# Regrouped element-wise work, reordered first loads and part of the relu moved to ScalarE in a fused sparse-attention, Fourier and MLP kernel

## The chip, the cores and the metric

The kernel runs on one core of one Trainium2 chip. The metric is device time in microseconds (us). A kernel is run several times; the text gives the median with the lowest and the highest run. A run counts as "slow" when it is more than 1.5% above the fastest of its kernel. Times are compared with the kernel before on the same chip; the traces come from several chips, and of the kernel before there is one.

Engines are written as in the profile: PE is the matrix engine (TensorE), PEld its weight loads, DVE is VectorE, ACT is ScalarE, POOL is GpSimd, SP is SyncE, and "q" after an engine means its queue of issued transfers.

## The reference

Sparse attention with a block gate, then a Fourier mix, a normalisation and an MLP. Cut to what matters:

```python
# q, k, v: batch 4, 8 heads, 768 positions, 64 wide; blocks of 64 positions, so 12 blocks
k_rep = k.reshape(B, H, 12, 64, D).mean(axis=3)
gate  = einsum('bhsd,bhnd->bhsn', q, k_rep)        # then -1e9 where the block lies ahead
sel   = top 3 blocks of gate per query, and the query's own block
scores = q @ k^T / 8, kept where the block is in sel and key <= query
x = softmax(scores) @ v                            # heads side by side: 4 x 768 x 512
u = x + real(fft over positions and features of x)
un = (u - mean(u)) / sqrt(var(u) + 1e-6)
out = u + relu(un @ w1) @ w2                       # w1: 512 x 2048, w2: 2048 x 512
```

## The kernel before

The program handles batches in a pipeline: while attention of batch *b* runs, the Fourier stage and the MLP of batch *b*-1 run beside it, and after batch 3 a tail without attention remains. Attention goes through head pairs. Stage A transposes q and k and forms sums of keys by block, stage B computes gate scores and the top-3 mask, stage C transposes the mask into extra rows of the query operand ("gate columns", 12 rows by 768), stage D computes scores, exponentials, the causal mask on diagonal tiles and the product with v. A scheduler decides the final order on each engine's queue, under the data dependencies; that order is called the built order below.

The loads of batch 0. Query and key tiles have two buffers. The weight loads of the MLP come from POOL behind a "gate": a copy of one element that can't run before pair 2's transposed query exists.

```python
def gen_weights():
    blk_src = attn_P[0][2]["qt"]                    # pair 2 of batch 0
    nc.gpsimd.tensor_copy(out=dummy1[0:1, 0:1], in_=blk_src[0:1, 0:1])   # the gate
    emit_fft_consts()
    for dt in range(NDT):
        nc.gpsimd.dma_start(out=w1_sb[:, dt, 0:DF // 2], ...)    # cut: second half, then w2

def emit_attn_dma(b, hp, ...):                      # cut: v
    qn = apool.tile([128, NST, 2, 64], FP, tag="q_nat", ...)     # the pool has two buffers
    kn = apool.tile([128, NST, 2, 64], FP, tag="k_nat", ...)
    eng = nc.scalar if (b == 0 and hp == 1) else nc.sync
```

The element-wise work of attention: key sums in stage A, the mask in stage B, the diagonal masks in stage D.

```python
# stage A, for each half g of the keys (tp = transposed keys in PSUM, both heads of a pair)
for e in range(2):
    nc.vector.tensor_reduce(out=kr24[64*e:64*e+64, 12*e+6*g:12*e+6*g+6],
                            in_=ps[64*e:64*e+64]..., op=add)
# stage B, for each head e
for st in range(NST):
    nc.vector.max(out=mx8[:, st, :], in_=gsb[:, st, NB*e:NB*(e+1)])
nc.vector.tensor_tensor(out=gm, in0=gsb..., in1=mx8[:, :, 2:3]..., op=is_ge)
nc.vector.tensor_tensor(out=gm, in0=gm, in1=own01, op=max)
nc.vector.tensor_scalar(out=gm, in0=gm, scalar1=1.0, scalar2=-NEG, op0=subtract, op1=mult)
# stage D, for each bank of scores
nc.scalar.activation(out=pt[:, po:po+wid_bank], in_=sp, func=AF.Exp, scale=0.125)
for dof in diags:                                   # each diagonal tile by itself
    nc.vector.tensor_tensor(out=pt[:, dof:dof+128], in0=pt[:, dof:dof+128], in1=ut01, op=mult)
```

The relu of the MLP, 16 times per batch, from PSUM:

```python
nc.vector.tensor_scalar(out=hT[it][:, 0:512],   in0=ha, scalar1=0.0, ..., op0=max)
nc.vector.tensor_scalar(out=hT[it][:, 512:768], in0=hb, scalar1=0.0, ..., op0=max)
```

The softmax here doesn't subtract the row's maximum and nothing guards it: scores larger than these inputs give would overflow.

## Time and profile before

The time was 430.17 us (426.59 to 431.02). The profiled run took 430.97 us, and its span is 429.2 us. The first lines are from the page of the kernel before: busy time of each engine, and the granted TensorE clock in 40 slices of 10.7 us, in tenths of full speed.

```profile
PE 359.6 (84%) x2638; PEld 229.9 (54%) x2638; DVE 313.2 (73%) x1079; ACT 169.7 (40%) x355; POOL 39.1 (9%) x59
PEclk9655555768957999999969999999789999989999
```

PE is busy for 84% of the span, but not always at full speed: slices three to seven stand near 5, half speed. The average also hides stages with different limits, so here is the windows view of the same kernel, cut at marks that the trace gives: first score, last product with v of batch 0, then batch 3's first half (until PE transposes the normalised rows, ahead of the MLP), its second half, and the tail. The columns are the window, its length, busy time and instruction count of PE, PEld, DVE, ACT and POOL, the granted clock, the DMA share and GB/s.

```profile
0.00:42.90 42.90, 22.33 (x100) 17.41 (x101) 15.60 (x78) 13.33 (x27) 19.47 (x35) 0.67 1.20 188
42.90:81.70 38.80, 37.01 (x285) 24.93 (x282) 24.87 (x119) 29.25 (x59) 4.92 (x6) 0.53 0.70 96
257.50:310.40 52.90, 44.48 (x278) 26.88 (x275) 44.77 (x158) 27.11 (x58) 1.34 (x2) 0.95 0.28 64
310.40:348.50 38.10, 37.74 (x380) 25.91 (x381) 32.48 (x107) 13.98 (x31) 0.00 (x0) 0.94 0.00 1
348.50:429.20 80.70, 70.98 (x400) 37.76 (x396) 45.91 (x98) 4.70 (x8) 0.00 (x0) 0.97 0.11 40
```

Four readings follow. The first 42.9 us are waiting for data: PE is busy for 22.3 of them. The stretch to 81.7 us is PE-bound at a clock of 0.53. In the first half of batch 3 PE stands still for 52.90 - 44.48 = 8.4 us. In the second half PE is busy for 37.7 of 38.1 us, so nothing that DVE or ACT does there can matter unless it makes PE wait.

What holds the first 42.9 us is in the chain of waits (the chain of work that ended last; start, length, what). Pieces of it up to the first exponential:

```profile
13.99 0.87 PE tp_0_0_0_192 L230 x3
...
16.81 0.37 SPq L179
...
17.23 16.78 DMA qn_2_179<-in_q_dram
...
34.14 0.87 PE tp_2_0_0_300 L230 x3
...
43.49 1.28 ACT L300
...
```

Pair 0's transposes start at 14.0 us. When they are done, SP issues pair 2's query load (line 179) into the freed buffer, and that load takes 16.8 us; pair 2's transposes start at 34.1 us. The 1.28 us on ACT is a table load right ahead of the first exponential (ACT_TABLE_LOAD, line 300, 1283 ns).

The view of PE's waits shows the wait for the gate columns, once per batch (line, waited for, us in total, times, longest):

```profile
PE tp_2_0_0_300 L230 <- DMA qn_2_179<-in_q_dram: 11.0, 1, 11.0
PE sc_1_0_0_1406 L293 <- DVE qg_1_0_1034 L276: 4.7, 1, 4.7
...
PE sc_1_0_0_3898 L293 <- DVE qg_1_0_3469 L276: 4.2, 1, 4.2
```

### The profile page before, as it was taken

The page shows a single profiled execution, that of the slowest core. Times are in us where ns is not written, and L with a number is a line of the kernel's source. Part 1 is how long each engine was busy: PE and PEld are TensorE (multiplying, and loading weights), DVE is VectorE, ACT ScalarE, POOL GpSimd, SP SyncE. Part 2 cuts the span into 40 slices and gives each one's busy share as a digit, 9 for nine tenths or more (in the row PEclk, how much of TensorE's full clock was granted, in tenths as well). Part 3 has the DMA queues.
Part 4 walks back from the last instruction along what each step waited for, and adds up shares of the span by engine and source line. Part 5 has one row for each costly group of instructions (what it writes and reads, how often), then busy time and mean ns, then how long its engine had stood idle before and what let it go on. Part 6 is the DMA issues. An engine that isn't in the chain of part 4 may idle for free.

```text
span 429.2 us, 7093 instructions
## 1 busy us (share of the span) xinstructions
PE 359.6 (84%) x2638; PEld 229.9 (54%) x2638; DVE 313.2 (73%) x1079; ACT 169.7 (40%) x355; POOL 39.1 (9%) x59
## 2 busy tenths in 40 slices
PE   6518999667659999998599998999599999959996
PEld 2417666445427666465456664666276655536542
DVE  0436666759896989688989889589979893777611
ACT  1513967736851440443763323635624402010000
POOL 6703012200001111000000111000000000000000
PEclk9655555768957999999969999999789999989999
DMA  9999972725302115444302227410000001100021
GB/s 159 213 201 180 195 106 19 96 43 120 74 0 20 13 9 37 124 124 99 98 2 20 19 20 118 122 51 25 2 2 1 2 2 73 52 23 2 0 75 73
DMA packets 84627, 28.04 MB, mean 65 GB/s; under 512 B 78032, under 2 KB 80304, under 8 KB 84592
## 3 DMA queue, kind: packets, MB, share of 16 engines
q0 software_dynamic: 28832, 8.48, 18.3%
q1 hardware_dynamic: 52416, 18.28, 17.7%
q10 hardware_dynamic: 3344, 0.82, 1.1%
q8 instruction: 21, 0.34, 0.3%
q14 instruction: 14, 0.11, 0.1%
HBM read 28.62 MB, written 6.29 MB: 81 GB/s over the span
## 4 chain that ended last, share of the span: by engine, by line
PE 67%; DVE 20%; DMA 7%; ACT 4%; issue 2%; SPq 0%; ACTq 0%
DMA qn_2_179<-in_q_dram 4%; DMA qn_1_137<-in_q_dram 2%; PE ch_5_3691 L481 1%; PE ch_5_2445 L481 1%; PE ch_5_5142 L481 1%; PE ch_5_4730 L481 1%; PE ch_4_4699 L481 1%; PE ch_3_5104 L481 1%; PE ch_2_5085 L481 1%; PE ch_0_5047 L481 1%; PE ch_3_4668 L481 1%; PE ch_2_4627 L481 1%; PE ch_0_4553 L481 1%; PE ch_4_3586 L481 1%; PE ch_3_3555 L481 1%
## 5 line engine op out<-in xcount | busy, mean ns | idle before, releaser
L466 PEld LDWEIGHTS <-w_sb 128*128 128x128 f16 x256 | 25.1, 98 | 25.7 <-issue 0.3
L467 PEld LDWEIGHTS <-w_sb 128*128 128x128 f16 x256 | 25.0, 98 | 6.0 <-issue 0.7
L188 POOL DMA_DIRECT2D v_0_0_89<-in_v_dram x4 | 3.4, 857 | 120.4 <-PE av_0_0_2736 L317 56.0
L293 PEld LDWEIGHTS <-kI_1_82 76*128 76x128 f16 x32 | 4.2, 134 | 14.3 <-issue 5.3
L230 PE MATMUL tp_2_0_0_300<-id_72,qn_2_179 128*128 128x128 f32 x3 | 0.9, 430 | 11.0 <-DMA qn_2_179<-in_q_dram 11.0
L140 ACT COPY unT_0_4797<-unt_0_4807 128x768 f16<-128x768 f16 x1 | 0.8, 798 | 20.3 <-PE unt_0_4807 L455 20.3
L293 PEld LDWEIGHTS <-kI_1_86 76*128 76x128 f16 x32 | 4.1, 130 | 8.6 <-issue 6.3
L121 PE MATMUL warmps<-warm_src 128*128 128x512 f16 x22 | 6.5, 467 | 1.2 <-DVE v_0_2_91 L131 1.2
L383 PE MATMUL yp_0_997<-fs_sb,fg_989 128*128 128x193 f16 x6 | 1.2, 364 | 7.7 <-DVE fg_989 L371 7.7
L383 PEld LDWEIGHTS <-fg_989 128*128 128x128 f16 x24 | 2.4, 117 | 8.7 <-DVE fg_989 L371 7.9
L394 ACT CAST yg_0_4606<-yp_0_4599 128x386 f16<-128x386 f32 x1 | 0.6, 598 | 15.0 <-PE yp_0_4599 L383 15.0
L188 POOL DMA_DIRECT2D v_0_1_90<-in_v_dram x4 | 3.3, 826 | 34.6 <-PE av_1_0_1721 L317 12.4
L230 PEld LDWEIGHTS tp_2_0_0_300<-id_72,qn_2_179 128*128 128x128 f32 x3 | 0.5, 212 | 11.1 <-issue 11.1
L235 DVE COPY qT_0_2_295<-tp_2_0_0_300 128x384 f32<-128x384 f32 x1 | 0.6, 557 | 8.0 <-PE tp_2_0_0_300 L230 8.0
L455 PE MATMUL unt_0_4807<-id_73,x_3300 128*128 128x128 f16 x6 | 1.7, 288 | 5.3 <-DVE x_3300 L448 5.3
L230 PE MATMUL tp_0_0_0_192<-id_72,qn_0_97 128*128 128x128 f32 x3 | 0.9, 430 | 6.2 <-DMA qn_1_137<-in_q_dram 6.2
L188 POOL DMA_DIRECT2D v_0_2_91<-in_v_dram x4 | 3.3, 828 | 28.7 <-PE av_2_0_3152 L317 10.8
L239 ACT CAST kI_2_83<-tp_2_1_0_314 64x384 f16<-64x384 f32 x1 | 0.5, 472 | 13.0 <-PE tp_2_1_0_314 L230 13.0
L235 DVE COPY qT_0_0_187<-tp_0_0_0_192 128x384 f32<-128x384 f32 x1 | 0.6, 558 | 6.9 <-PE tp_0_0_0_192 L230 6.9
L236 ACT CAST qg_0_0_188<-tp_0_0_0_192 64x384 f16<-64x384 f32 x1 | 0.5, 472 | 12.7 <-DMA kn_1_138<-in_k_dram 12.7
L455 PEld LDWEIGHTS <-x_3300 128*128 128x128 f16 x24 | 2.1, 130 | 6.3 <-DVE x_3300 L448 5.8
L239 ACT CAST kI_0_81<-tp_0_1_0_2124 64x384 f16<-64x384 f32 x1 | 0.5, 472 | 12.0 <-PE tp_0_1_0_2124 L230 12.0
(2598 smaller groups left out, 1347.3 us busy)
## 6 DMA issues: line engine op xcount, KB each, us to landing
w_sb<-in_moe_w_ch_dram POOLq DMA_DIRECT2D x8, 256.0 KB, 10.4
w_sb<-in_moe_w_ch_dram POOLq DMA_DIRECT2D x4, 512.0 KB, 13.5
out_dram<-u_939 SPq DMA_DIRECT2D x6, 256.0 KB, 2.4
out_dram<-u_2071 SPq DMA_DIRECT2D x6, 256.0 KB, 2.0
out_dram<-u_3317 SPq DMA_DIRECT2D x6, 256.0 KB, 2.0
out_dram<-u_4546 SPq DMA_DIRECT2D x6, 256.0 KB, 2.0
fs_sb<-c_FS POOLq DMA_DIRECT2D x1, 582.0 KB, 6.5
qn_0_97<-in_q_dram SPq DMA_DIRECT2D x4, 96.0 KB, 4.7
```

What stands on the lines that cost most here:

```text
L121: nc.tensor.matmul(wps, wsrc[:, 0:128], wsrc, start=True, stop=True)
L140: eng.copy(out=dst, in_=src)
L188: nc.gpsimd.dma_start(out=v16_t[e][sl][:, :, 0:64], in_=v[b, h].rearrange("(jt p) d -> p jt d", p=128))
L230: nc.tensor.transpose(ps[:, i, :], src[:, st, :, :].rearrange("p h d -> p (h d)"), id32)
L235: nc.vector.tensor_copy(out=qt[:, cols], in_=flat)
L239: nc.scalar.copy(out=kI[0][0:64, cols], in_=flat[0:64])
L293: nc.tensor.matmul(sp[:, co:co + (a1 - a0)], kI[e][0:76, 128 * jt:128 * (jt + 1)], qg[e][0:76, a0:a1], start=True, stop=True)
L383: nc.tensor.matmul(out_p, fg[:, 3 * par + st, 128 * g:128 * (g + 1)], fs_sb[:, g % 2, par, st, 0:KQ], start=(st == 0), stop=(st == 2))
L455: nc.tensor.transpose(tps[:, st, :], un16[:, st, 128 * dt:128 * (dt + 1)], id16)
L466: nc.tensor.matmul(ha, w1s, unT[dt][:, 0:512], start=(dt == 0), stop=(dt == NDT - 1))
L467: nc.tensor.matmul(hb, w1s, unT[dt][:, 512:768], start=(dt == 0), stop=(dt == NDT - 1))
L481: nc.tensor.matmul(cps, hT[it][:, 128 * st:128 * (st + 1)], w2_sb[:, it, :], start=(it == 0), stop=(it == NIT - 1))
```

## The change

Its intent is to start attention earlier, to take work from DVE by doing the same element-wise work in fewer and larger instructions, and to give ACT two thirds of the relu (512 of 768 columns). The core of the diff (cut: constants, pools, index bookkeeping):

```diff
 # loads
-            qn = apool.tile([128, NST, 2, 64], FP, tag="q_nat", name=...)      # and kn
-            eng = nc.scalar if (b == 0 and hp == 1) else nc.sync
+            qn = apool.tile([128, NST, 2, 64], FP, tag="q_nat", name=..., bufs=3)
+            # q on SP's queue, k on ACT's queue in batch 0; pairs 0, 1, 2 issued up front
-    emit_attn_dma(0, 0, qk_only=True)
     emit_priority_consts()
-    emit_attn_dma(0, 1, qk_only=True)
+    for hp in range(3):
+        emit_attn_dma(0, hp, qk_only=True)
+    emit_rest_consts()
 # key sums: both heads in one reduce, then spread by a 0/1 table
-                        for e in range(2):
-                            nc.vector.tensor_reduce(out=kr24[64*e:64*e+64, ...], ...)
+                        nc.vector.tensor_reduce(out=kr12[:, 6*g:6*g+6], in_=ps..., op=add)
+            nc.vector.tensor_tensor(out=kr24..., in0=kr12...to_broadcast([128, 2, NB]),
+                                    in1=half24..., op=mult)
 # top-3 mask: both heads at once, two operations for six
-                nc.vector.tensor_tensor(out=gm, ..., op=is_ge)
-                nc.vector.tensor_tensor(out=gm, in0=gm, in1=own01, op=max)
-                nc.vector.tensor_scalar(out=gm, ..., op0=subtract, op1=mult)
+            nc.vector.tensor_tensor(out=g4, in0=g4, in1=mx8[..., 2:3]..., op=is_lt)
+            nc.vector.scalar_tensor_tensor(out=gmp..., in0=g4, scalar=NEG, in1=other24...,
+                                           op0=mult, op1=mult)
 # scores: diagonal tiles side by side, so that one multiply masks up to four
-        [(0, 0, 512)],
-        [(0, 512, 768), (4, 512, 768)],                              # cut
+        [(0, 0, 128), (1, 128, 256), (2, 256, 384), (3, 384, 512)],
+        [(4, 512, 640), (5, 640, 768), (4, 640, 768), (0, 128, 256)],  # cut
-                    for dof in diags:
-                        nc.vector.tensor_tensor(out=pt[:, dof:dof+128], ..., in1=ut01, op=mult)
+                    if ndiag:
+                        nc.vector.tensor_tensor(out=dg, in0=dg,
+                            in1=ut01...to_broadcast([128, ndiag, 128]), op=mult)
 # relu of the first 512 columns
-            nc.vector.tensor_scalar(out=hT[it][:, 0:512], in0=ha, scalar1=0.0, ..., op0=max)
+            nc.scalar.activation(out=hT[it][:, 0:512], in_=ha, func=AF.Relu)
```

More of the change, by code (lines that the diff above doesn't have):

```diff
@@ L54, in _consts_np @@
     cz24 = np.concatenate([cz, cz], axis=1)
-    own01 = ((s // 64)[:, None] == nn[None, :]).astype(np.float16)
+    other = ((s // 64)[:, None] != nn[None, :]).astype(np.float32)
+    other24 = np.concatenate([other, other], axis=1)
+    half24 = ((jj[:, None] // 64) == (np.arange(2 * NB)[None, :] // NB)).astype(np.float32)
     IndR = (nn[:, None] == (s[None, :] // 64)).astype(np.float16)
     return dict(FS=FS, FD=FD, ident32=ident32, ident16=ident16,
-                ltri=ltri, ut01=ut01, cz24=cz24, own01=own01, IndR=IndR)
+                ltri=ltri, ut01=ut01, cz24=cz24, other24=other24, half24=half24, IndR=IndR)
 @with_exitstack
@@ L90 @@
     bpool = ctx.enter_context(tc.tile_pool(name="bat", bufs=1))
-    spool = ctx.enter_context(tc.tile_pool(name="small", bufs=8))
+    spool = ctx.enter_context(tc.tile_pool(name="small", bufs=4))
     def pst(shape, name, dtype=FP, tag="ps", bufs=None):
@@ L101 @@
     cz24 = cpool.tile([128, NST, 2 * NB], FP, tag="c_cz24", name="cz24")
-    own01 = cpool.tile([128, NST, NB], F16, tag="c_own", name="own01")
+    other24 = cpool.tile([128, NST, 2 * NB], FP, tag="c_other", name="other24")
+    half24 = cpool.tile([128, 2 * NB], FP, tag="c_half", name="half24")
     eps1 = cpool.tile([128, 1], FP, tag="c_eps1", name="eps1")
@@ L113, in emit_priority_consts @@
         nc.sync.dma_start(id32, dr["ident32"].ap())
-        nc.sync.dma_start(id16, dr["ident16"].ap())
+        nc.gpsimd.dma_start(id16, dr["ident16"].ap())
         nc.vector.memset(eps1, 1e-6)
@@ L124, in emit_rest_consts @@
     def emit_rest_consts():
-        nc.sync.dma_start(cz24, dr["cz24"].ap().rearrange("(st p) n -> p st n", p=128))
-        nc.sync.dma_start(own01, dr["own01"].ap().rearrange("(st p) n -> p st n", p=128))
-        nc.scalar.dma_start(ut01, dr["ut01"].ap())
+        nc.gpsimd.dma_start(cz24, dr["cz24"].ap().rearrange("(st p) n -> p st n", p=128))
+        nc.gpsimd.dma_start(half24, dr["half24"].ap())
+        nc.gpsimd.dma_start(other24, dr["other24"].ap().rearrange("(st p) n -> p st n", p=128))
+        nc.gpsimd.dma_start(ut01, dr["ut01"].ap())
         for e in range(2):
@@ L168, in emit_attn_dma @@
         if not v_only:
-            qn = apool.tile([128, NST, 2, 64], FP, tag="q_nat", name=f"qn_{b}_{hp}")
-            kn = apool.tile([128, NST, 2, 64], FP, tag="k_nat", name=f"kn_{b}_{hp}")
-            eng = nc.scalar if (b == 0 and hp == 1) else nc.sync
-            nsp = 2 if (b == 0 and hp < 2) else 1
-            for e in range(2):
-                h = 2 * hp + e
-                for part in range(nsp):
-                    s0, s1 = part * (NST // nsp), (part + 1) * (NST // nsp)
-                    eng.dma_start(qn[:, s0:s1, e, :],
-                                  q[b, h, 128 * s0:128 * s1].rearrange("(st p) d -> p st d", p=128))
-                    eng.dma_start(kn[:, s0:s1, e, :],
-                                  k[b, h, 128 * s0:128 * s1].rearrange("(st p) d -> p st d", p=128))
+            qn = apool.tile([128, NST, 2, 64], FP, tag="q_nat", name=f"qn_{b}_{hp}", bufs=3)
+            kn = apool.tile([128, NST, 2, 64], FP, tag="k_nat", name=f"kn_{b}_{hp}", bufs=3)
+            for (t, src, eng) in ((qn, q, nc.sync), (kn, k, nc.scalar if b == 0 else nc.sync)):
+                for e in range(2):
+                    eng.dma_start(t[:, :, e, :], src[b, 2 * hp + e]
+                                  .rearrange("(st p) d -> p st d", p=128))
             P.setdefault(hp, {})["qn"] = qn
@@ L191 @@
     BANKS = [
-        [(0, 0, 512)],
-        [(0, 512, 768), (4, 512, 768)],
-        [(1, 128, 640)],
-        [(1, 640, 768), (3, 384, 768)],
-        [(2, 256, 768)],
-        [(5, 640, 768)],
+        [(0, 0, 128), (1, 128, 256), (2, 256, 384), (3, 384, 512)],
+        [(4, 512, 640), (5, 640, 768), (4, 640, 768), (0, 128, 256)],
+        [(0, 256, 768)],
+        [(1, 256, 768)],
+        [(2, 384, 768), (3, 512, 640)],
+        [(3, 640, 768)],
     ]
-    OFF = {}
+    COL = {}
     PT_W = 0
@@ L202 @@
         for (jt, a0, a1) in bank:
-            if jt not in OFF:
-                OFF[jt] = PT_W - (a0 - 128 * jt)
+            for i in range(a0, a1, 128):
+                COL[jt, i // 128] = PT_W + i - a0
             PT_W += a1 - a0
-    assert PT_W == 2688
+    assert PT_W == 2688 and len(COL) == 21
     def gen_attention(b):
@@ L217, in stage_A @@
             qt = apool.tile([128, S], FP, tag="qT32", name=f"qT32_{b}_{hp}")
-            qg = [apool.tile([128, S], F16, tag=f"qg{e}", name=f"qg_{b}_{hp}_{e}", bufs=4)
+            qg = [apool.tile([128, S], F16, tag=f"qg{e}", name=f"qg_{b}_{hp}_{e}", bufs=3)
                   for e in range(2)]
@@ L221, in stage_A @@
             kr24 = apool.tile([128, 2 * NB], FP, tag="kr24", name=f"kr24_{b}_{hp}")
-            nc.vector.memset(kr24, 0.0)
+            kr12 = apool.tile([128, NB], FP, tag="kr12", name=f"kr12_{b}_{hp}")
             d["qt"], d["qg"], d["kI"], d["kr24"] = qt, qg, kI, kr24
@@ L240, in stage_A @@
                         nc.scalar.copy(out=kI[1][0:64, cols], in_=flat[64:128])
-                        for e in range(2):
-                            nc.vector.tensor_reduce(
-                                out=kr24[64 * e:64 * e + 64, 12 * e + 6 * g:12 * e + 6 * g + 6],
-                                in_=ps[64 * e:64 * e + 64].rearrange("p a (x c) -> p a x c", x=2),
-                                axis=mybir.AxisListType.X, op=mybir.AluOpType.add)
+                        nc.vector.tensor_reduce(
+                            out=kr12[:, 6 * g:6 * g + 6],
+                            in_=ps.rearrange("p a (x c) -> p a x c", x=2),
+                            axis=mybir.AxisListType.X, op=mybir.AluOpType.add)
+            nc.vector.tensor_tensor(out=kr24.rearrange("p (e n) -> p e n", e=2),
+                                    in0=kr12.rearrange("p (o n) -> p o n", o=1)
+                                    .to_broadcast([128, 2, NB]),
+                                    in1=half24.rearrange("p (e n) -> p e n", e=2),
+                                    op=mybir.AluOpType.mult)
         def stage_B(hp):
@@ L254, in stage_B @@
             nc.vector.tensor_tensor(out=gsb, in0=gps, in1=cz24, op=mybir.AluOpType.add)
-            gmp = apool.tile([128, NST, 44], F16, tag="gmp", name=f"gmp_{b}_{hp}", bufs=4)
+            gmp = apool.tile([128, NST, 64], F16, tag="gmp", name=f"gmp_{b}_{hp}", bufs=4)
             d["gmp"] = gmp
-            for e in range(2):
-                gm = gmp[:, :, 32 * e:32 * e + NB]
-                mx8 = spool.tile([128, NST, 8], FP, tag="mx8", name=f"mx8_{b}_{hp}_{e}")
-                for st in range(NST):
-                    nc.vector.max(out=mx8[:, st, :], in_=gsb[:, st, NB * e:NB * (e + 1)])
-                nc.vector.tensor_tensor(out=gm, in0=gsb[:, :, NB * e:NB * (e + 1)],
-                                        in1=mx8[:, :, 2:3].to_broadcast([128, NST, NB]),
-                                        op=mybir.AluOpType.is_ge)
-                nc.vector.tensor_tensor(out=gm, in0=gm, in1=own01, op=mybir.AluOpType.max)
-                nc.vector.tensor_scalar(out=gm, in0=gm, scalar1=1.0, scalar2=-NEG,
-                                        op0=mybir.AluOpType.subtract, op1=mybir.AluOpType.mult)
+            mx8 = spool.tile([128, NST, 2, 8], FP, tag="mx8", name=f"mx8_{b}_{hp}", bufs=4)
+            for st in range(NST):
+                for e in range(2):
+                    nc.vector.max(out=mx8[:, st, e, :], in_=gsb[:, st, NB * e:NB * (e + 1)])
+            g4 = gsb.rearrange("p s (e n) -> p s e n", e=2)
+            nc.vector.tensor_tensor(out=g4, in0=g4,
+                                    in1=mx8[:, :, :, 2:3].to_broadcast([128, NST, 2, NB]),
+                                    op=mybir.AluOpType.is_lt)
+            nc.vector.scalar_tensor_tensor(
+                out=gmp.rearrange("p s (e n) -> p s e n", e=2)[:, :, :, 0:NB], in0=g4, scalar=NEG,
+                in1=other24.rearrange("p s (e n) -> p s e n", e=2),
+                op0=mybir.AluOpType.mult, op1=mybir.AluOpType.mult)
         def stage_C(hp):
@@ L273, in stage_C @@
             for st in range(NST):
-                nc.tensor.transpose(gt[0:44, st, :], gmp[:, st, :], id16)
+                nc.tensor.transpose(gt[0:44, st, :], gmp[:, st, 0:44], id16)
             for e in range(2):
@@ L290, in stage_D_scores @@
                     co = 0
-                    diags = []
+                    ndiag = 0
                     for (jt, a0, a1) in bank:
@@ L297, in stage_D_scores @@
                         if a0 == 128 * jt:
-                            diags.append(po + co)
+                            ndiag += 1
                         co += a1 - a0
@@ L301, in stage_D_scores @@
                                          scale=0.125)
-                    for dof in diags:
-                        nc.vector.tensor_tensor(out=pt[:, dof:dof + 128], in0=pt[:, dof:dof + 128],
-                                                in1=ut01, op=mybir.AluOpType.mult)
+                    if ndiag:
+                        dg = pt[:, po:po + 128 * ndiag].rearrange("p (n c) -> p n c", c=128)
+                        nc.vector.tensor_tensor(
+                            out=dg, in0=dg,
+                            in1=ut01.rearrange("p (o c) -> p o c", o=1)
+                            .to_broadcast([128, ndiag, 128]),
+                            op=mybir.AluOpType.mult)
                 po += wid_bank
@@ L317, in stage_D_av @@
                         nc.tensor.matmul(av[:, st, 0:65],
-                                         pt[:, OFF[jt] + 128 * (st - jt):OFF[jt] + 128 * (st - jt) + 128],
+                                         pt[:, COL[jt, st]:COL[jt, st] + 128],
                                          v16[e][:, jt, 0:65],
@@ L328, in gen_attention @@
         if b > 0:
-            emit_attn_dma(b, 0, qk_only=True)
-            emit_attn_dma(b, 1, qk_only=True)
-            emit_attn_dma(b, 0, v_only=True)
-            emit_attn_dma(b, 1, v_only=True)
+            for hp in range(3):
+                emit_attn_dma(b, hp, qk_only=True)
+            for hp in range(3):
+                emit_attn_dma(b, hp, v_only=True)
             yield
@@ L335, in gen_attention @@
             if i < NP:
-                if i + 2 < NP:
+                if 1 <= i and i + 2 < NP:
                     emit_attn_dma(b, i + 2)
@@ L467, in gen_post @@
                 nc.tensor.matmul(hb, w1s, unT[dt][:, 512:768], start=(dt == 0), stop=(dt == NDT - 1))
-            nc.vector.tensor_scalar(out=hT[it][:, 0:512], in0=ha, scalar1=0.0, scalar2=None,
-                                    op0=mybir.AluOpType.max)
+            nc.scalar.activation(out=hT[it][:, 0:512], in_=ha, func=AF.Relu)
             nc.vector.tensor_scalar(out=hT[it][:, 512:768], in0=hb, scalar1=0.0, scalar2=None,
@@ L498, in drive @@
             gens = alive
-    emit_attn_dma(0, 0, qk_only=True)
     emit_priority_consts()
-    emit_attn_dma(0, 1, qk_only=True)
+    for hp in range(3):
+        emit_attn_dma(0, hp, qk_only=True)
+    emit_rest_consts()
     emit_attn_dma(0, 0, v_only=True)
     emit_attn_dma(0, 1, v_only=True)
-    emit_rest_consts()
+    emit_attn_dma(0, 2, v_only=True)
     def gen_weights_delayed(nskip):
```

## The prediction

> **What bounds the kernel now.** The span (429.2 us), from the windows view and the chain of waits:
>
> - 0 to 44 us, loads. The first transposes start at 14.0 us; those of head pair 2 wait for its query load (16.8 us in the chain) until 34.1. That load starts only when pair 0's buffer is free, and shares the DMA engines with the MLP weights.
> - 44 to 80 us, attention of batch 0: PE busy 36.2 of 38 us at granted clock 0.53.
> - 80 to 166, 166 to 257, 257 to 348 us: attention of batch b beside Fourier and MLP of b-1. Each has a first half (batch 3: 51.5 us, PE 43.2, DVE 43.4 busy) whose chain alternates between DVE and PE, and a second half (39.5 us, PE 39.0) that is PE alone. Batch 1's first half is DVE-bound (DVE 40.0 of 46, PE 27.2).
> - 348 to 429 us, tail without attention: PE, a short DVE chain, PE.
>
> **What the change does.** The Fourier stage does not change. The rest:
>
> 1. Loads: the identity first, q and k on two queues, three buffers, so pair 2 is fetched at once. In the built order the weight gate now stands before all eight first weight loads (before, seven stood ahead of it). At the 160 to 210 GB/s of the first slices (estimate), pair 0 lands near 7 us, pair 2 near 17, pair 3 near 23. PE's order still puts pair 3's transposes before the first score, so scores start near 25 instead of 43.5 us. The 36.7 us after that keep their length if the clock stays low. Gain 18 us.
> 2. Key sums: 64 reduces of 553 ns become 32 plus 16 small multiplies: about 4 us of DVE per batch. Masks: 192 multiplies of 220 ns become 64; from 128 columns 220 ns, 762 columns 553, 1536 columns 954 I estimate 420 ns (512 columns) and 290 (256). [...] Top-k mask: six operations become two. Together 6 us of DVE per batch in the first halves, about 4 of it in the chain. Gain 4 us each for batches 2 and 3, 5 for batch 1.
> 3. Relu: 64 x 690 ns go from DVE to ACT (about 600 ns each, by exponentials of that size). [...] the built order keeps two table loads. It lies in the PE-bound half and gains almost nothing; relus beside bursts of twelve exponentials (one per 0.48 us) may stall PE 0.5 us a burst. Cost 1 to 2 us in all.
> 4. Scores: 8 matmuls per head become 13, most 128 columns wide; one takes 54 ns start to start, so no loss.
>
> The tail stays at 81 us.
>
> **Predicted: 400 us**, 389 to 412 in 8 of 10 cases. Faster by over 2%: 0.97; within 2%: 0.025; slower: 0.005.
>
> **What would show it.** Step 1: first score near 25 us, batch 0 ending near 62. Step 2: DVE busy down from 313 to 235-250 us (relu included), PE's 4.2 us wait for the gate columns shorter, first halves about 47 us. Step 3: ACT busy near 205 us, second halves 39 to 41 us, short new waits of PE on ACT's relu.
>
> **What would make it wrong.** The clock: it stood at half speed from 32 to 90 us although PE was busy; at full clock batch 0 would end up to 8 us earlier. Pair 3's load or the values could come late. Relu behind exponentials could cost more.

430 us, less 18 for the loads and 13 for the element-wise work (5 + 4 + 4), plus 1 to 2 for the relu, comes to 400 to 401. Its 420 and 290 ns for grouped masks are the estimate from the three durations it names; these lie near 155 ns plus 0.52 ns per column.

## More of the kernel before

The chain at the end of batch 3's first half is a chain on DVE. These pieces lie between the gate scores (PE, line 251) and the first of the diagonal masks behind them:

```profile
299.20 1.27 PE g_2_3811 L251 x12
...
302.51 0.45 DVE kr_3_3_3779 L242
302.97 0.56 DVE kr_3_3_3779 L242
303.54 0.55 DVE kr_3_3_3779 L242
304.11 0.56 DVE kr_3_3_3779 L242
...
304.97 0.56 DVE qg_1_0_3469 L276
...
307.49 0.11 DVE ptl_1_0_3896 L303
```

The four key-sum reduces (line 242) take 0.45 to 0.56 us each, one after the other, ahead of the gate columns (qg, line 276) that PE's scores wait for. The diagonal masks (ptl, line 303) contribute five pieces of 0.11 to 0.13 us. Over the whole of this first half, key sums take 5.4 us of the chain (summed over its pieces).

## The result, and the profile after

The changed kernel took 399.54 us (398.69 to 406.64, four runs); the kernel before took 428.83 us (426.59 to 431.02) beside it. The ratio is 0.932 (95% interval 0.926 to 0.938). Ratios here and below are the mean time of one kernel's fast runs over that of the other's fast runs of the same rounds, so not quite the ratio of the quoted medians.

The first profile of the changed kernel fell in a slow run (406.64 us, mean clock 0.873; the fast runs had 0.90). The comparison below uses a profile of the same kernel in a fast run (398.40 us, clock 0.903), taken in a later set of runs. The page's busy times and clock in that run:

```profile
PE 351.8 (89%) x2798; PEld 231.1 (58%) x2798; DVE 244.4 (62%) x791; ACT 203.9 (51%) x419; POOL 42.5 (11%) x64
PEclk9655997985799999997799999997799999989999
```

DVE lost 68.8 us and ACT gained 34.2 us. The clock row has fewer fives early on. The windows view of this kernel, cut at the same marks:

```profile
0.00:27.60 27.60, 22.61 (x100) 16.32 (x101) 11.16 (x65) 13.35 (x27) 17.12 (x31) 0.73 1.37 180
27.60:58.90 31.30, 28.15 (x325) 21.52 (x322) 19.20 (x74) 26.95 (x59) 10.57 (x15) 0.80 1.23 213
227.60:277.20 49.60, 44.12 (x294) 27.85 (x292) 39.27 (x131) 26.82 (x58) 1.29 (x2) 0.95 0.23 53
277.20:315.70 38.50, 38.26 (x401) 26.87 (x402) 21.58 (x64) 22.95 (x47) 0.00 (x0) 0.93 0.01 1
315.70:396.60 80.90, 70.95 (x398) 37.77 (x396) 36.11 (x82) 14.26 (x24) 0.00 (x0) 0.97 0.11 40
```

The gain lies in three places. The first score comes 15.3 us earlier. The stretch after it is 7.5 us shorter, at a clock of 0.80 where it was 0.53. The first half of batch 3 is 3.3 us shorter, of which 2.9 us is less standing still of PE (49.60 - 44.12 = 5.5 us in place of 8.4). The second half and the tail moved by 0.4 and 0.2 us, although DVE is 10.9 us less busy in that second half: this PE-bound stage did not notice. Summed over the span: batch 0 gave 22.8 us (its end moved from 81.7 to 58.9), batches 1 to 3 gave 10.0 (266.8 to 256.8), the tail took 0.2.

The chain of waits at the start, for the changed kernel:

```profile
2.83 8.80 DMA qn<-in_q_dram
...
14.82 2.55 PE g L253 x12
...
20.28 0.47 DVE kr L239
...
21.70 2.59 PE g L253 x12
...
29.16 1.28 ACT L303
...
```

No load stands in the chain after 11.6 us. From there it is transposes, gate scores and copies, with PE at half clock: the twelve gate-score passes take 2.55 us here, where the clock row stands at 6 and 5, and 1.27 us at full clock (in the chain of batch 3, and as long in the kernel before, at a granted clock of 1.00 from 299.2 to 300.5 us). And the end of batch 3's first half:

```profile
267.43 1.27 PE g L253 x12
...
269.69 0.87 DVE mx L262 x12
270.59 0.55 DVE qg L279
271.17 0.56 DVE kr L239
...
271.94 0.47 DVE kr L239
...
272.73 0.56 DVE qg L279
...
273.34 3.83 PE sc L296 x18
```

Two key-sum reduces stand where four stood, and PE starts its scores 4.6 us after the gate scores ended (5.1 us before). Over the whole first half, key sums take 1.7 us of the chain where they took 5.4. PE's waits for gate columns are now several short ones (7 times, 2.1 us the longest; their sum fell from 15.1 to 10.4 us), and the wait for pair 2's query is gone; what is left of waiting for queries is 2.0 us:

```profile
PE sc L296 <- DVE qg L279: 10.4, 7, 2.1
PE tp L228 <- DMA qn<-in_q_dram: 2.0, 1, 2.0
PE sc L296 <- ACT ptl L303: 1.9, 2, 1.7
```

### The profile page after: what moved, and what is told of

It is laid out like the page before. It is cut to its first block, busy times and chain, and to the rows that moved or that the text cites. A ratio compares the mean times of both kernels' runs of the same rounds, so it can differ in the third digit from the quotient of the medians.

```text
span 404.9 us, 7205 instructions
## 1 busy us (share of the span) xinstructions
PE 358.5 (89%) x2798; PEld 236.2 (58%) x2798; DVE 244.7 (60%) x791; ACT 205.5 (51%) x419; POOL 42.5 (11%) x64
## 4 chain that ended last, share of the span: by engine, by line
PE 74%; DVE 13%; ACT 5%; DMA 4%; issue 2%; POOL 0%; ACTq 0%; SPq 0%; POOLq 0%
DMA cz_75<-c_cz 2%; DMA kI_1_87<-c_IndR 2%; DMA qn_0_2017<-in_q_dram 1%; PE ch_5_3624 L487 1%; PE ch_1_3339 L487 1%; PE ch_5_2394 L487 1%; PE ch_1_2109 L487 1%; PE ch_5_5072 L487 1%; PE ch_5_4660 L487 1%; PE ch_2_5015 L487 1%; PE ch_4_5053 L487 1%; PE ch_3_5034 L487 1%; PE ch_1_4996 L487 1%; PE ch_0_4977 L487 1%; PE ch_4_4629 L487 1%
## 5 line engine op out<-in xcount | busy, mean ns | idle before, releaser
L296 PEld LDWEIGHTS <-kI_1_83 76*128 76x128 f16 x52 | 5.5, 131 | 8.9 <-issue 3.6
L296 PEld LDWEIGHTS <-kI_1_87 76*128 76x128 f16 x52 | 5.2, 128 | 7.8 <-DVE qg_1_1_1012 L279 2.4
L296 PEld LDWEIGHTS <-kI_0_86 76*128 76x128 f16 x52 | 4.9, 112 | 3.4 <-issue 2.7
L186 POOL DMA_DIRECT2D v_0_2_92<-in_v_dram x4 | 3.3, 822 | 28.0 <-PE av_2_0_1868 L324 10.9
L296 PEld LDWEIGHTS <-kI_2_88 76*128 76x128 f16 x52 | 4.6, 108 | 2.7 <-issue 1.2
L296 PEld LDWEIGHTS <-kI_3_89 76*128 76x128 f16 x52 | 4.6, 107 | 2.2 <-issue 0.7
L296 PEld LDWEIGHTS <-kI_0_82 76*128 76x128 f16 x52 | 5.0, 114 | 1.4 <-issue 0.9
L124 PEld LDWEIGHTS <-warm_src 128*128 128x128 f16 x22 | 2.6, 121 | 5.1 <-issue 2.7
L296 PEld LDWEIGHTS <-kI_3_85 76*128 76x128 f16 x52 | 4.7, 108 | 1.2
L296 PEld LDWEIGHTS <-kI_2_84 76*128 76x128 f16 x52 | 4.6, 108 | 1.3 <-issue 0.2
L228 PE MATMUL tp_1_0_0_228<-id_72,qn_1_134 128*128 128x128 f32 x3 | 0.9, 430 | 4.4 <-DMA qn_1_134<-in_q_dram 4.4
```

Of the source, the lines that this page charges most:

```text
L124: nc.tensor.matmul(wps, wsrc[:, 0:128], wsrc, start=True, stop=True)
L186: nc.gpsimd.dma_start(out=v16_t[e][sl][:, :, 0:64], in_=v[b, h].rearrange("(jt p) d -> p jt d", p=128))
L228: nc.tensor.transpose(ps[:, i, :], src[:, st, :, :].rearrange("p h d -> p (h d)"), id32)
L296: nc.tensor.matmul(sp[:, co:co + (a1 - a0)], kI[e][0:76, 128 * jt:128 * (jt + 1)], qg[e][0:76, a0:a1], start=True, stop=True)
```

## The experiments

The total was near what was predicted, so the question was whether its parts were. The theory was the prediction's: 18 us from the loads, 13 from the element-wise work, a small cost from the relu. The main rivals were that the loads give less than that and the element-wise work more; that the loads gain by no longer sharing the DMA engines with the MLP's weights, not by being issued earlier; and that a large part is the clock of batch 0, which is not the change's doing at all. All runs gave correct results. This table collects what the traces of the profiled runs show; "first score" is the time of PE's first score, "stretch" is from there to the end of batch 0, "batches 1-3" is their sum, all in us.

| kernel | median time | before, same chip | first score | stretch | end of batch 0 | batches 1-3 | tail |
|---|---|---|---|---|---|---|---|
| before | 428.83 | - | 42.9 | 38.8 | 81.7 | 266.8 | 80.7 |
| changed (after_third) | 398.53 | 428.21 | 27.6 | 31.3 | 58.9 | 256.8 | 80.9 |
| changed (its first profile, slow) | 399.54 | 428.83 | 30.3 | 35.6 | 65.8 | 257.0 | 82.1 |
| loads_only | 420.31 | 428.72 | 31.9 | 37.5 | 69.4 | 267.6 | 81.7 |
| gate_only | 421.00 | 428.21 | 33.4 | 37.3 | 70.8 | 267.1 | 81.4 |
| elem_again | 411.23 | 428.21 | 36.9 | 34.5 | 71.4 | 257.5 | 80.6 |
| kr_only | 418.03 | 428.21 | 40.0 | 37.6 | 77.6 | 258.7 | 82.4 |
| diag_only | 423.47 | 427.90 | 42.5 | 30.2 | 72.7 | 268.4 | 80.7 |
| relu_only | 428.35 | 428.72 | 42.5 | 33.0 | 75.5 | 266.3 | 82.3 |
| no_relu | 399.53 | 428.86 | 28.9 | 31.1 | 60.1 | 256.9 | 80.9 |
| after_ungated | 404.89 | 427.90 | 28.1 | 35.6 | 63.6 | 256.9 | 82.1 |
| c_first_exp | 394.43 | 427.90 | 22.7 | 34.2 | 56.9 | 254.4 | 82.6 |

Of the columns, the first score and batches 1-3 are steady where kernels share the code that sets them (for instance 266.3 to 268.4 in all kernels without the new key sums). The stretch is not: 33.0 in relu_only and 38.8 in the kernel before, which have the same code there; the granted clock of the stretch is 0.79 in the one and 0.53 in the other.

### The changed kernel again, loads alone, element-wise work alone, relu alone

after_again is the changed kernel without an edit.

> The changed kernel unchanged, for a profile in the fast state (the first one fell in a slow run of 406.6 us against 398.7 to 400.3). Both theories: 397 to 401 us. If the 7 us between its slow and fast runs is the clock of TensorE in batches 0 and 1, the fast profile shows the same order of work and the same waits, with fewer half-speed stretches before 140 us; if it is the DMA, the first score comes earlier than 30.3 us.

The median was 398.23 us against 428.72 us. Three runs took 397.6 to 398.5 us, and the fourth, which was the profiled one, 428.55 us at a mean clock of 0.787. In that run the clock was not lost early only: from 107 us to the end of the program its clock row stands at 8 in every slice but three (5, 5 and 6), where the fast profile mostly has 9, and the 512-column matmuls of the MLP take 419 to 422 ns on average in place of 379. PE is busy for 384.0 us in place of 351.8, DVE and ACT for 246.2 and 203.8 in place of 244.4 and 203.9. It shows how far a lower clock can carry the time with the same code, up to the time of the kernel before; it says nothing on the change. Because of it the interval of the ratio was wide (0.936, 0.920 to 0.952), and the kernel was run once more below.

loads_only has the part of the diff that concerns loads (three buffers, q and k on two queues, pairs 0 to 2 up front, constants on POOL's queue), with the old element-wise work and relu:

```diff
-            qn = apool.tile([128, NST, 2, 64], FP, tag="q_nat", name=...)
+            qn = apool.tile([128, NST, 2, 64], FP, tag="q_nat", name=..., bufs=3)
+    for hp in range(3):
+        emit_attn_dma(0, hp, qk_only=True)      # and the other load edits of the change
```

> The kernel before with the new loads alone (one load per head, q and k on two queues, constants on the third, three buffers). Theory: the loads give 12 to 15 us: about 415 us, first score near 30 us instead of 42.9, batch 0 over near 67 us instead of 81.4, and the three batches and the tail keep their lengths (85, 91, 91, 81 us). Rival (batch 0 is bound by TensorE at half clock, so an earlier start is given back): at most 5 us, 424 us or more.

It took 420.31 us (420.05 to 420.56) against 428.72: 8.4 us by medians. The ratio is 0.988 with an interval that includes 1 (0.971 to 1.004), because only two of the seven runs of the kernel before counted as fast. The result lies between the theory and its rival, as the median gain is 8.4 us where 12 to 15 or at most 5 were expected. The trace is clear where the clock of the stretch doesn't enter: the first score comes at 31.9 us in place of 42.9. Batches 1 to 3 did not move (267.6 against 266.8). Why the first score comes 4.3 us later than in the changed kernel, with the same loads, is in the chain of waits of loads_only:

```profile
2.84 9.47 DMA qn<-in_q_dram
...
14.47 0.54 DVE kr L236
15.03 0.56 DVE kr L236
...
16.89 2.74 PE g L245 x12
...
```

No load stands in it after 12.3 us. Up to the first exponential it holds eight old key-sum reduces (4.4 us in all), where the changed kernel's chain holds one new one of 0.47 us.

elem_only has the new key sums, mask and diagonal grouping, with the old loads of q, k and v and the old relu (the diff of the change's second, third and fourth part; it also loads the new constants and keeps the change's smaller pools):

```diff
+                        nc.vector.tensor_reduce(out=kr12[:, 6*g:6*g+6], in_=ps..., op=add)
+            nc.vector.tensor_tensor(out=g4, in0=g4, in1=mx8[..., 2:3]..., op=is_lt)
+            nc.vector.scalar_tensor_tensor(out=gmp..., op0=mult, op1=mult)
+                        nc.vector.tensor_tensor(out=dg, in0=dg, in1=ut01...to_broadcast(...), op=mult)
```

> The kernel before with the regrouped attention element-wise work alone (key sums, top-k mask, score banks with grouped diagonals); old loads, relu on DVE. Theory: about 3 us in each of batches 1 to 3 and 2 us in batch 0, 417 to 420 us, DVE busy near 285 us. Rival (the batches became shorter because relu left DVE): 426 us or more.

Three runs took 408.6 to 413.5 us, faster than the 417 to 420 expected. The fourth, the profiled one, took 685.07 us: the mean of the 512-column matmuls was 677 to 680 ns where it is 379 ns in the changed kernel's fast profile. Its trace holds no clock record (the page has no clock row, and the 1.0 listed for the run is what the tool gives without one), so it doesn't show what clock was granted. It can't be compared with anything, and the same kernel went again as elem_again.

relu_only moves the relu of 512 columns to ACT and does nothing else:

```diff
-            nc.vector.tensor_scalar(out=hT[it][:, 0:512], in0=ha, scalar1=0.0, ..., op0=max)
+            nc.scalar.activation(out=hT[it][:, 0:512], in_=ha, func=AF.Relu)
```

> The kernel before with two thirds of the relu on ACT alone. Theory: the relu lies in the halves that PE bounds, so nothing is gained: 427 to 431 us, DVE busy near 272 us, ACT near 206 us. Rival (DVE relieved of 40 us is the gain of the batches): 420 us or less.

It took 428.35 us against 428.72 (ratio 1.007, 0.991 to 1.023). One relu takes 691 ns on DVE and 625 ns on ACT. The windows view of relu_only, the second half of batch 3:

```profile
303.70:341.80 38.10, 37.81 (x380) 25.95 (x381) 24.09 (x91) 22.86 (x47) 0.00 (x0) 0.94 0.00 1
```

DVE fell from 32.5 to 24.1 us and ACT rose from 14.0 to 22.9, and the window is 38.10 us as it was, with PE busy for 37.8. The time is the one that the theory gave. The feared stall of PE behind ACT did not appear: no wait on the relu is among PE's waits in that profile.

### The fast profile, element-wise work again, key sums alone, and the weight gate alone

after_third is the changed kernel once more.

> The changed kernel once more, for a profile of a fast run (two profiles fell in slow ones). Theory: its fast runs (397 to 400 us) differ from the first profile (404.9 us) by the clock in batch 0: the scores of batch 0 then last about 30 us instead of 35.6, the halves of batches 1 to 3 are the same as there within 0.5 us. Rival: the difference is in the tail or in the loads.

It took 398.53 us (398.40 to 399.25) against 428.21, ratio 0.933 (0.926 to 0.940). Its profile is the one shown in the result. The theory, that only the clock of batch 0 sets the slow profile apart, holds in part: of the 8.3 us between the two spans, 4.3 lie in the stretch (clock 0.58 against 0.80), but 2.6 lie before the first score and 1.2 in the tail.

elem_again is the kernel of elem_only.

> The element-wise part alone once more, as its profile fell in a run of 685 us with all matmuls slowed. It gave 17 us where 9 to 12 were expected. Theory A: the halves of batches 1 to 3 shorten by 3.3 us each as in the whole change, and the rest comes in batch 0, where the weight gate of the built order now stands after four weight loads instead of seven, so that pair 2's queries land about 4 us earlier, and where a higher clock is granted: batch 0 ends near 74 us instead of 81.7. Theory B: the regrouping itself is worth more than thought: batches 1 to 3 shorten by 5 us each or more.

It took 411.23 us (409.16 to 414.53), ratio 0.963 (0.955 to 0.972): 17.0 us by medians. Theory A fits the trace. Batches 1 to 3 gave 9.3 us (266.8 to 257.5). And batch 0 gave 10.3 us (81.7 to 71.4), with no edit in the code of the q, k, v and weight loads. Of these, 6.0 lie before the first score (36.9 us in place of 42.9) and 4.3 in the stretch, at a clock of 0.60 in place of 0.53. Most of the 6.0 goes with the built order of POOL's queue. In the kernel before, seven weight loads stand ahead of the gate; in this one, four. Pair 2's transposes start at 29.6 us in place of 34.1. An edit in DVE's work thus changed how many transfers compete with pair 2's query.

kr_only has the new key sums alone:

```diff
-                        for e in range(2):
-                            nc.vector.tensor_reduce(out=kr24[64*e:64*e+64, ...], ...)
+                        nc.vector.tensor_reduce(out=kr12[:, 6*g:6*g+6], in_=ps..., op=add)
+            nc.vector.tensor_tensor(out=kr24..., in0=kr12..., in1=half24..., op=mult)
```

> The kernel before with the key sums alone changed (one reduce for both heads and a masking multiply). Theory: two thirds of the gain of the regrouping in the batches: first halves of batches 2 and 3 at 50.5 to 51 us instead of 52.9. The weight gate stands after five loads, so pair 2 should come 2 to 3 us earlier: 419 to 424 us. If the halved number of reduces meant nothing: first halves 52.9 us as before.

It took 418.03 us (416.18 to 420.69), ratio 0.977 (0.967 to 0.987). Batches 1 to 3 take 258.7 us, so the key sums alone give 8.1 of the 10.0 us that the whole change gives there. That leaves about 1 us for the top-k mask and the diagonals together (elem_again: 257.5); the mask was not run alone. In the chain of batch 3's first half, key sums fell from 5.4 to 1.2 us. The windows view, batch 3's first half in kr_only:

```profile
247.60:297.70 50.10, 43.71 (x275) 27.00 (x274) 40.25 (x151) 26.54 (x57) 1.27 (x2) 0.96 0.29 68
```

PE stands still for 6.4 us where it stood for 8.4. The half is 50.1 us long, a little less than the 50.5 to 51 expected. Five weight loads stand ahead of the gate here, and pair 2's transposes start at 31.6 us.

gate_only keeps the old loads, with two buffers and the old order, and makes the gate hold. In the kernel before, the weight loads share no data with the gate's copy, so the scheduler may put them ahead of it. Here POOL copies one element of pair 2's transposed query into each tile that a weight load then overwrites, so each load has to come after:

```diff
-        nc.gpsimd.tensor_copy(out=dummy1[0:1, 0:1], in_=blk_src[0:1, 0:1])
+        for dt in range(NDT):
+            for c in (0, DF // 2):
+                nc.gpsimd.tensor_copy(out=w1_sb[0:1, dt, c:c + 1], in_=blk_src[0:1, 0:1])
+        for c in range(4):
+            nc.gpsimd.tensor_copy(out=w2_sb[0:1, 4 * c, 0:1], in_=blk_src[0:1, 0:1])
```

> The kernel before with one thing changed: every load of the MLP weights really waits for pair 2's queries to be transposed. Theory (contention): pair 2's queries land by 24 us instead of 34, the first score starts near 33 us instead of 42.9, about 419 us. Rival (the late issue for want of a third buffer is the cause): pair 2's transposes still start after 31 us, 426 us or more.

It took 421.00 us (414.74 to 422.26), ratio 0.978 (0.963 to 0.993). Its profiled run is labelled slow, being 1.5% above a single fast run of 414.74 us; its clock (0.869) is that of most runs of the kernel before (0.86 to 0.87), so it is a fair trace to read loads from. The chain of waits of gate_only:

```profile
17.19 0.37 SPq L183
...
17.61 7.07 DMA qn<-in_q_dram
24.81 2.17 PE tp L234 x9
...
34.16 1.28 ACT L304
...
```

The issue stands where it stood (17.2 us; 16.8 before), into the same two buffers. The load takes 7.07 us where it took 16.78, as the theory of contention said. The gain of gate_only (7.2 us) and that of loads_only (8.4 us) are the same within the spread of the runs. So what held pair 2 back was mainly competition with the weights for the DMA engines (in the kernel before, the DMA share is 1.08 while the load runs, from 17.2 to 34.0 us, at 225 GB/s): with the weights away, its transposes start at 24.8 us in place of 34.1. The late issue after pair 0's buffer cost less: with the new loads alone they start at 20.0 us, and the first score comes 1.5 us ahead of gate_only's (31.9 against 33.4). The weights are issued by POOL and the query by SP, so in these two traces separate queues did not keep them apart. Across the two-buffer kernels, the start of pair 2's transposes follows the number of weight loads ahead of the gate: 33.7 to 34.1 us with seven (three kernels), 31.6 with five, 29.6 with four, 24.8 with none.

### Diagonals alone, the change without its gate, and a version meant to be faster

diag_only has the regrouped score banks and the grouped diagonal masks alone:

```diff
-        [(0, 0, 512)],
-        [(0, 512, 768), (4, 512, 768)],                              # cut
+        [(0, 0, 128), (1, 128, 256), (2, 256, 384), (3, 384, 512)],
+        [(4, 512, 640), (5, 640, 768), (4, 640, 768), (0, 128, 256)],  # cut
-                    for dof in diags: ...                            # 6 multiplies per head
+                    if ndiag: ...                                    # 2 multiplies per head
```

> The kernel before with the score banks and the grouped diagonal masks alone (192 masks of 220 ns become 64). The key sums gave 2.8 of the 3.2 us per batch, so theory: DVE busy falls by 10 us or more and nothing is gained in the batches: first halves 52.3 to 52.9 us, second halves 38 to 38.6, at most 1 us slower from the narrower score matmuls. What moves in batch 0 is the weight gate's place in the built order (seven loads before it, as in the kernel before), so 425 to 430 us. Rival (the prediction: all DVE work of the first halves counts alike): first halves near 51.5 us.

It took 423.47 us (422.39 to 424.84), ratio 0.990 (0.983 to 0.997). The windows view, batch 3's first half in diag_only:

```profile
250.10:302.80 52.70, 44.34 (x295) 27.88 (x292) 44.60 (x149) 26.85 (x58) 1.34 (x2) 0.95 0.28 65
```

DVE lost 10.5 us in all (313.2 to 302.7), but 0.2 us in this window, and the window is 52.70 us where it was 52.90. Batches 1 to 3 together are 1.6 us longer than before, not shorter; the lengthening is in batch 1's first half (48.3 in place of 46.5 us), at a clock of 0.67 in place of 0.77. As expected, then, nothing is gained in the batches; that the total came out under the 425 to 430 us expected is due to the stretch of batch 0 (30.2 in place of 38.8 us), at a clock of 0.80 in place of 0.53. All four runs of diag_only have that clock (0.877 to 0.884, against 0.853 to 0.893 before). Whether the regrouping causes it is open.

after_ungated is the changed kernel without the gate:

```diff
-        blk_src = attn_P[0][2]["qt"]
-        nc.gpsimd.tensor_copy(out=dummy1[0:1, 0:1], in_=blk_src[0:1, 0:1])
```

> The changed kernel without the gate of the weight loads. The gate alone gave the kernel before all that the new loads gave it. Theory: with three buffers the queries of pair 2 are issued at 2 us, before any weight load can start (near 18 us on its queue), so only pair 3 can suffer: first score 27.6 to 30 us, 398 to 402 us. Rival (the gate is the gain): first score after 33 us, 405 us or more.

It took 404.89 us (399.91 to 405.40), ratio 0.944 (0.937 to 0.950). The first score is at 28.1 us, against 27.6. But the run is no test of the gate: with the constants and the values ahead of them on POOL's queue, the first weight load is issued at 22.6 us without the gate and at 22.3 with it, and pair 2's transposes start at 17.7 and 17.8 us, earlier than either. So the gate did not hold anything back in the changed kernel, and whether an early issue would do with the weights issued at 16 us, as in the kernel before, no run shows. The time missed the 398 to 402 us expected. The 6 us are in the stretch: 35.6 us against 31.3, at a clock of 0.58 against 0.80:

```profile
28.10:63.60 35.50, 33.44 (x324) 25.82 (x322) 19.24 (x74) 28.48 (x59) 10.58 (x15) 0.58 1.30 207
```

The changed kernel's own first profile has the same 35.6 us, and one run of after_ungated (399.91 us, clock 0.904) was as fast as the changed kernel. So both kernels can land in either case, although their loads are the same in time; three of four runs of after_ungated landed in the slower one, and one of twelve of the changed kernel (406.64 us; its 428.55 us run is left out). Why is open.

c_first_exp is the changed kernel with two edits. Stage C is emitted ahead of stages A and B of the same step, so that the gate columns of a pair do not queue on DVE behind the key sums of a later pair. And the early dummy activation is Exp in place of Ln, so that the exponential's table is loaded while the first loads run, not right ahead of the first exponential:

```diff
-        nc.scalar.activation(out=dummy1, in_=eps1, func=AF.Ln, bias=eps1)
+        nc.scalar.activation(out=dummy1, in_=eps1, func=AF.Exp)
         for i in range(NP + 3):
+            if 0 <= i - 2 < NP:
+                stage_C(i - 2)
             if i < NP:
                 ...
                 stage_A(i)
             if 0 <= i - 1 < NP:
                 stage_B(i - 1)
-            if 0 <= i - 2 < NP:
-                stage_C(i - 2)
```

> The changed kernel with two small edits: in each step the gate columns of an older head pair are emitted before the transposes and the gate scores of younger pairs, and the first dummy activation is an exponential, so one table load instead of two. Theory: the waits of the first scores of pair 1 for the gate columns (1.6 and 1.5 us per batch) go, 1 to 3 us per batch; in batch 0 the scores no longer stand behind pair 3's transposes, first score near 22 us, and 1.3 us of table load leave the chain: 385 to 393 us. Rival (the first half is bound by the chain of statistics on DVE, the wait was slack): 394 to 398 us.

It took 394.43 us (393.40 to 396.07, six runs), ratio 0.922 (0.918 to 0.927). It is the fastest kernel, about 4 us under the changed one by medians (of different sets of runs). That is outside the 385 to 393 us of the theory and inside the rival's range, though what the rival said, that the wait was slack, is only partly so. The first score comes at 22.7 us, as the theory had it, and batches 1 to 3 take 254.4 us in place of 256.8. PE's waits in c_first_exp:

```profile
PE sc L296 <- ACT ptl L303: 9.0, 8, 2.3
```

The waits of scores for gate columns (10.4 us in the changed kernel) are gone from the view, and waits for exponentials took most of their place (9.0 us, 1.9 before). That fits the small gain: removing 10.4 us of waiting moved batches 1 to 3 by 2.4 us. The two edits were not run apart; but in the changed kernel the table load (29.2 us) came after the first score (27.6), so the earlier first score must come from the new order. The table load did leave the chain: no piece of 1.28 us stands ahead of its first exponentials (27.7 us), and ACT counts 418 instructions in place of 419.

### The change without the relu

no_relu is the changed kernel with the relu back on DVE (the diff of relu_only, reversed).

> The changed kernel with the relu back on DVE. The parts alone gave 8.4 (loads), 17 (element-wise) and 0.4 us (relu), 26 of the 30 us of the whole. Theory: relu is worth nothing in the whole either, the missing 4 us are loads and regrouping helping each other in batch 0: 397 to 401 us, or 404 to 406 where batch 0 falls back to half clock, second halves 37.6 to 38.6 us. Rival (relu pays once the first halves are shorter): 403 us or more with second halves above 39 us.

It took 399.53 us (398.88 to 400.14), ratio 0.931 (0.927 to 0.934); the changed kernel has 398.53 and 0.933. In the second half of batch 3, DVE is busy for 30.2 us where it is 21.6 with the relu on ACT, and that half is 38.3 us in place of 38.5. As expected, moving the relu is worth nothing measurable, in the old kernel or in the new one.

## Why the prediction was right or wrong

The time was right: 400 predicted, 399.54 measured, and the direction with it. The split that led to it was not, and its errors cancelled: that the total came so near is in part luck.

- **Loads, -18 us: too large.** Loads alone gave 8.4 us by medians. The step that failed was the sum behind "scores start near 25 instead of 43.5 us", taken over whole: alone, the new loads bring the first score to 31.9 us. By the chains of waits, most of the 4.3 us to the changed kernel's 27.6 are element-wise work: the chain of loads_only holds 4.4 us of old key sums there, where the changed kernel's holds 0.5, and no load after 12.3 us. The landing times were estimated well: pairs 0, 2 and 3 were to land near 7, 17 and 23 us, and their transposes start at 8.2, 17.8 and 25.0 us in the changed kernel. What was missing is that from about 15 us on, the chain is work on PE, DVE and ACT at half clock (2.55 us for gate scores that take 1.27 at full clock), so the first score is at 27.6 us, not 25.
- **What the loads gain by.** The prediction named both causes of the late pair 2: the wait for pair 0's buffer and the shared DMA engines. The gate_only run shows that removing the second one by itself brings nearly the whole gain of the loads (7.2 of 8.4 us). That the gate's place matters in the kernel before was read correctly; in the changed kernel it does not, as after_ungated has the same times of loads without it. That the place also moves when DVE's work is edited was not seen.
- **Element-wise work, -13 us in batches 1 to 3: near, and mis-sized.** Batches 1 to 3 gave 10.0 us. Each first half lost 3.2 to 3.3 us (46.5 to 43.2, 52.9 to 49.6, 52.8 to 49.6), where 5, 4 and 4 were predicted. Of this, key sums gave 8.1 us. The grouped diagonals, counted as part of the 6 us of DVE per batch of which about 4 lay in the chain, gave nothing there: they held 0.6 us of the chain of batch 3's first half, against 5.4 for the key sums, and diag_only shortened that half by 0.2 us. So the step that was mis-sized is "about 4 of it in the chain": 3.3 us per batch were gained, nearly all by the key sums. The costs of single operations were right: 420 and 290 ns predicted for grouped masks, 416 and 287 measured.
- **Element-wise work in batch 0: left out.** The prediction gave it no gain in batch 0. Alone it gave 10.3 us there, with the gate's place in the order and with the clock, and beside the new loads it takes 4 us of key sums out of the chain ahead of the first score.
- **"The 36.7 us after that keep their length if the clock stays low": the condition failed.** In the fast profile of the changed kernel the stretch is 31.3 us at a clock of 0.80. In the slow run that was profiled first it is 35.6 us. The prediction named this as its main risk, with "up to 8 us earlier"; the fast profile shows batch 0 ending at 58.9 us, 3 us ahead of the predicted 62. It also gave the half-speed time as 32 to 90 us. That was a misreading of the clock record's origin, which lies 10.5 us away from the span's start; the page's clock row puts it near 22 to 80 us. PE was busy for 45.4 of these 58 us, at a granted clock of 0.50, and its gate scores took 2.54 us there against 1.27 at full clock.
- **Relu, +1 to 2 us: wrong in size.** It cost nothing: relu_only stands at 428.35 against 428.72, and no_relu at 399.53 against 398.53. No wait of PE on ACT's relu appeared, and no further table load (two in relu_only, 1283 ns each, as in the kernel before). That it would gain nothing in a PE-bound half was right, and second halves were 37.6 to 38.5 us as before (38.0 to 38.4); the predicted 39 to 41 came from cutting the halves at other marks and from that cost.
- **Busy times and waits: right.** DVE 244.4 us (235 to 250 predicted), ACT 203.9 (near 205), the wait of 4.2 us for gate columns broken into shorter ones, tail 80.9 (81).

The parts' medians add up to 8.4 + 17.0 + 0.4 = 25.8 us; the whole gave 29.7. In the traces the batch-0 gains of loads and element-wise work add up well (12.3 + 10.3 = 22.6, whole 22.8), but with different clocks in each, so the agreement proves little. The remaining 4 us are of the size of the clock's play in batch 0, where the stretch went from 30.2 to 38.8 us across profiles. What decides when TensorE's clock rises there is the one thing that stays open; no run varied it on purpose. The work in the stretch alone doesn't decide it, as relu_only, with the same work there, had 0.79 where the kernel before had 0.53.

## What to carry to other kernels

A gate in front of bulk loads holds only if data ties each load to it; otherwise the scheduler decides, and an edit elsewhere can move it, so look at the built order and at how long the small critical load takes (16.8 us against 7.1 here). Count what an edit removes from the chain, not from an engine's busy time: 8 us came from the key sums, which stood in the chain ahead of what PE waited for (5.4 us in one first half), and nothing from removing 10 us of diagonal masks or from moving 44 us of relu. Before an edit is said to test something, look whether it changed anything in the trace: taking the gate out of the changed kernel moved no load. A total that comes out right is no proof of its parts: run each part alone, with the kernel before on the same chip.
